# Another order for the steps of a fused attention and maxout kernel

## Chip, cores and metric

The kernel runs on one core of a Trainium2 chip. The time is the device time of one execution in microseconds. In the program one order of steps is written out by hand for all engines: TensorE (PE, with its weight loads as PEld), VectorE (DVE), ScalarE (ACT), GpSimd (POOL, here almost only an issuer of transfers) and SyncE (SP, an issuer of transfers).

## What is computed

Eight sequences of 448 positions go through attention with twelve heads of 64, and the result through a feed-forward block whose two branches are combined by a maximum.

```python
def _attn_ref(q, k, v, cap):            # (8, 12, 448, 64) each
    scores = q @ k^T / sqrt(64)
    scores = cap * tanh(scores / cap)
    attn = exp(scores - max);  attn = attn / (sum(attn) + 1e-9)
    return attn @ v

def _moe_ref(x, w1, w2, w_out):         # x: (3584, 768), w1, w2: (768, 1024)
    g = np.maximum(x @ w1, x @ w2)
    return g @ w_out                    # (3584, 768)
```

## The kernel before

**The arithmetic.** A maximum of two branches is h2 + relu(h1 - h2). So the kernel forms wd = w1 - w2 once on VectorE (steps `sub`) and wm = w2 · w_out once on TensorE (twelve products "premultiply", groups 0 to 11, from w2 transposed on TensorE by the steps W), and then computes relu(x · wd) · w_out + x · wm. Because tanh bounds the scores, exp is taken without a maximum.

**Tiles.** Four heads of one batch make a quad t; there are 24 quads, three for each batch. Quad 2 is cut into two parts of 256 and 192 queries, so there are 25 items n. Keys go in three tiles of 128 and a leftover of 64. Quads 0 to 4 are transposed on TensorE (steps X, copied by XC); quads 5 to 23 by the crossbar in a DMA that SyncE issues (`cr t`, line L373). kqs holds four quads of k and q as loaded, qkT three quads transposed, vp and vl four quads of v.

**The order.** One text, ORDER, lists 1,911 steps; each name stands for a function that issues one or more instructions. An engine takes its own instructions in the sequence in which they stand there, and waits in place for what they need; instructions of different engines are tied by semaphores alone. So the place of a step matters only among the steps of the same engine and queue. The steps:

| step | what it does | engine, line |
|---|---|---|
| lk, lq, lv, lw1, lw2, lwo | load k, q, v, the weights | POOL queue, L277, L284, L302, L317, L320, L307 |
| ld0, ld1, cd, cd1 | first loads of k and q, and their casts | SP and ACT queues; DVE, ACT |
| D | warming matmuls | PE L336 |
| X, Xh / XC | transposes on TensorE, and their copy to qkT | PE L365 / DVE L370 |
| W / WC | transposes of w2, and their copy | PE L344 / DVE L348 |
| cr t | crossbar transpose of quad t | SP queue, L373 |
| S n s z / T | scores of item n, sixth s, into PSUM slot z / tanh | PE L438 / ACT L447 |
| L n z / TL | leftover scores / their tanh | PE L456 / ACT L462 |
| E | exp, in place, of several tiles | ACT L469 |
| A, B | sums of exponentials over tiles | DVE L479, L484 |
| Y n bank / Yi 1 to 3 | totals / transpose, reciprocal, transpose | PE L497, L499, L502 / DVE L509, L512, L515 |
| VL, V | leftover values, values | PE L529, L539 |
| N n 0, N n 1 | normalise into xT | DVE L554, L558 |
| O g bank | group g takes a PSUM bank (no instruction) | |
| M x y n | n steps of groups x and y side by side | PE L582 |
| M x x n | n steps of group x on the whole array | PE L577 |
| H g | hand-over of group g | DVE queue, L590 |
| ev g | copy of a finished group out of PSUM | DVE L600, L613, L648, L651 |
| st b t | store of output tile t of batch b | SP and ACT queues, L622, L624, L629, L652 |

**Groups.** Group 12 and those behind it are stage 1 (x · wd, relu into gT) and stage 2 (gT · w_out + x · wm, copied to osb) of the batches in turn. In `M x y n` the two groups run in the upper and the lower 64 rows of the array at once; a group has to go through both halves, and between the two the kernel puts a hand-over, an empty instruction of VectorE that waits for the last matmul of the first half and is waited for by the first one of the second:

```python
    def hand_over(self, eng):
        self.turn = eng.nop().ins
        tc.add_manual_dep(self.turn, self.last[1].name, BANK, reason="bank")
```

The array works in different tilings: 64 x 128 for S and `M x y`, 64 x 32 for L and VL, 128 x 32 for Y and V, 64 x 64 for X, 128 x 128 for D, W and `M x x`.

**Buffers.** There are eight PSUM banks: two slots of two banks, z = 0 and 1, for scores and values (S, L and VL take them in turn; T, TL or N n 1 frees them), and four banks for groups, totals and transposes. Output tiles go through four buffers, `osb_all[:, (7 * (b // 2) + t) % OB, :DM]` with OB = 4, so a copy ev into one waits until the store of the tile four before has landed. `cr t` needs the buffer of qkT that was allocated three quads before, and quad t loaded in kqs.

**Ends.** ScalarE's work ends some 40 us before the kernel does; what is left then is stage 1 and 2 of the last batches on TensorE, with the last batch's 16 groups as `M x x`.

Of the kernel before, what the change touches and what calls it, by code (L numbers as in the profile page):

```python
# [14 lines left out]
lv 1 2; lq 6 0; lv 2 2; lw2 1; VL 0 1; W 2 2; WC 2; W 3 3; ev 1; WC 3; D 0 8; lq 5 0; E 0 1 0 2; E 0 0 0 3; Y 0 0;
Yi 0 1; Yi 0 2; Yi 0 3; lv 0 1; lv 0 0; lv 1 0; V 0 0; V 0 1; N 0 0; N 0 1; T 1 0; E 1 0 0 3; S 2 0 0; T 2 0;
E 1 1 2 4; E 1 1 0 2; O 2 2; O 3 1; M 2 3 8; H 3; H 2; lw2 2; W 4 3; WC 4; W 5 0; WC 5; M 3 2 3; lv 3 3; lk 5 0;
X 5 3; M 3 2 5; XC 5; S 2 1 0; lw1 0; sub 1 0; ev 3; L 2 1; TL 2; T 2 1; Y 1 0; Yi 1 1; Yi 1 2; sub 0 0; S 2 2 1;
T 2 2; E 2 1 0 2; O 4 3; O 5 1; M 4 5 8; H 5; lv 1 3; lv 1 1; VL 1 0; V 1 0; V 1 1; S 3 1 1; T 3 1; H 4; M 5 4 1;
ev 2; Yi 1 3; N 1 0; N 1 1; M 5 4 5; E 2 1 2 4; M 5 4 2; ev 5; S 3 0 1; T 3 0; lv 2 1; lq 8 0; lwo 1 0; O 6 0; O 7 2;  # L20
M 6 7 3; lk 6 0; M 6 7 1; lwo 1 1; M 6 7 2; S 3 2 0; T 3 2; M 6 7 2; H 7; H 6; ev 4; X 6 1; XC 6; L 3 1; TL 3;
E 3 1 0 2; lw1 1; sub 3 0; lk 10 0; lk 7 0; lv 3 2; lv 2 3; lv 2 0; lq 7 0; lk 8 0; lw1 2; lk 10 1; lq 10 0; lk 11 0;
lk 9 0; lk 11 1; lq 11 0; cr 5; lv 3 1; lq 9 0; lk 12 0; M 7 6 6; S 4 2 0; T 4 2; M 7 6 2; O 8 3; O 9 1; M 8 9 1;
ev 6; sub 2 0; ev 7; S 4 0 1; T 4 0; M 8 9 7; H 8; H 9; S 4 1 0; T 4 1; E 4 0 0 3; Y 2 0; Yi 2 1; Yi 2 2; VL 2 1;
X 7 2; XC 7; lk 12 1; lq 12 0; lk 13 0; lk 13 1; lq 13 0; lv 4 0; lv 4 1; lv 4 2; lv 4 3; lk 14 0; lv 3 0; lk 14 1;
lq 14 0; lk 15 0; lk 15 1; lq 15 0; X 8 0; XC 8; Yi 2 3; V 2 0; V 2 1; N 2 0; N 2 1; S 4 3 0; T 4 3; E 3 1 2 4;
M 9 8 8; ev 8; O 10 2; O 11 0; M 10 11 2; S 4 5 0; T 4 5; S 4 4 1; T 4 4; sub 5 0; M 10 11 6; H 11; H 10; sub 4 0;
ev 9; Y 3 3; Yi 3 1; S 5 2 0; T 5 2; M 11 10 4; S 5 0 1; T 5 0; M 11 10 4; Yi 3 2; ev 11; ev 10; L 4 0; TL 4; cr 6;
X 9 1; S 5 1 1; T 5 1; E 4 1 0 2; O 13 3; M 13 -1 2; O 14 0; M 13 14 4; O 17 2; M 17 14 2; XC 9; S 5 4 0; H 13;
M 17 13 3; H 14; M 17 13 1; M 14 13 2; VL 3 1; V 3 0; V 3 1; T 5 4; lv 5 0; lv 5 1; lv 5 2; lv 5 3; lk 16 0; lk 16 1;  # L30
lq 16 0; lk 17 0; lk 17 1; lq 17 0; lv 6 0; lv 6 1; lv 6 2; lv 6 3; lk 18 0; A 4 0 1; A 4 0 2; H 17; M 14 17 4; ev 13;
Yi 3 3; N 3 0; O 15 1; M 15 17 2; ev 17; O 19 3; M 15 19 4; H 15; N 3 1; E 4 1 2 4; L 5 0; TL 5; O 12 2; M 12 19 2;
H 19; M 12 15 4; H 12; M 19 15 2; ev 14; ev 15; A 4 1 1; S 5 3 1; T 5 3; E 5 1 0 2; M 19 12 4; ev 19; M -1 12 1;
O 18 0; M 18 12 1; O 16 1; M 18 16 5; H 18; M -1 16 1; H 16; S 5 5 0; cr 7; T 5 5; E 5 0 0 3; ev 12; M -1 18 1;
# [701 lines left out]
```

## Time and profile before

| | us |
|---|---|
| runs, median of 3 | 328.62 (328.51 to 330.5) |
| profiled execution, its own time | 329.16 |
| its span | 327.4 |
| TensorE busy | 319.1 (97%) |
| ScalarE busy | 274.5 (84%) |
| VectorE busy | 244.7 (75%) |
| GpSimd busy, nearly all of it issuing transfers | 163.5 (50%) |
| mean granted TensorE clock | 0.994 |

The span runs from the first to the last instruction; the execution's own time has 1.8 us around it. A busy row says that an instruction of the engine was under way, not that the engine ran at its peak. All times inside the span count from its start.

### The profile page before, as it was taken

To read this page: it belongs to the slowest core of one execution; us is meant where nothing else is said; L and a number is where in the kernel's file an instruction comes from. 1 tells how busy PE (TensorE), PEld (TensorE's weight loads), DVE (VectorE), ACT (ScalarE), POOL (GpSimd) and SP (SyncE) were. 2 spreads that over 40 slices of the span, in tenths; PEclk is the share of its full clock that TensorE was granted. 3 is DMA by queue.
4 is the path that set the end of the run, shared out by engine and by line. 5 is a ranking of instruction groups with operands and counts; after the bars stand their busy time and mean duration, and the time that the engine had idled before them with its cause. 6 is when DMAs were issued, how large, how long until landed. Compare 5 with 4: busy or idle time off the path is not lost.

```text
span 327.4 us, 10010 instructions
## 1 busy us (share of the span) xinstructions
PE 319.1 (97%) x4288; PEld 194.0 (59%) x4288; DVE 244.7 (75%) x447; ACT 274.5 (84%) x245; POOL 163.5 (50%) x241
## 2 busy tenths in 40 slices
PE   7799999999999999999999999999999999999995
PEld 7465567665546656555565565675567568555552
DVE  2349898988888688978888678889788777886213
ACT  3999999999999999999999998999899988900000
POOL 7567589998995865565577387543202000000000
PEclk9899999999999999999999999999999999999999
DMA  8999999999999999999999999996963006003034
GB/s 201 197 230 253 271 159 171 156 175 186 165 161 126 207 139 111 188 190 90 149 152 185 165 191 172 131 75 101 203 150 46 2 0 194 3 2 94 4 96 144
DMA packets 135083, 46.13 MB, mean 141 GB/s; under 512 B 116224, under 2 KB 130688, under 8 KB 134656
## 3 DMA queue, kind: packets, MB, share of 16 engines
q0 software_dynamic: 95168, 24.85, 76.9%
q1 hardware_dynamic: 39184, 19.40, 27.9%
q10 hardware_dynamic: 688, 1.25, 1.1%
q8 instruction: 33, 0.54, 0.7%
q14 instruction: 10, 0.08, 0.1%
HBM read 47.45 MB, written 11.01 MB: 179 GB/s over the span
## 4 chain that ended last, share of the span: by engine, by line
PE 94%; ACT 3%; DVE 2%; issue 0%; DVEq 0%
PE mm L582 59%; PE s L438 9%; PE s L539 9%; PE mm L577 8%; ACT e L447 2%; PE s L456 2%; PE s L529 2%; PE mm L502 2%; PE mm L336 2%; PE mm L365 1%; PE mm L497 1%; ACT e L469 0%; DVE xT L558 0%; PE mm L344 0%; ACT e L462 0%
## 5 line engine op out<-in xcount | busy, mean ns | idle before, releaser
L469 ACT ACTIVATE e<-e 128x1792 bf16<-128x1792 bf16 (+4 forms) x73 | 140.2, 1932 | 0.5
L447 ACT ACTIVATE e<-s 128x896 bf16<-128x896 f32 (+2 forms) x144 | 124.1, 935 | 6.0 <-PE s L438 5.7
L582 PE MATMUL mm<-wo_sb,gT 64*128 64x384 bf16 x768 | 95.8, 323 | 0.0
L582 PE MATMUL mm<-xT,wd_sb 64*128 64x448 bf16 (+2 forms) x768 | 79.9, 326 | 0.0
L582 PE MATMUL mm<-wm_sb,xT 64*128 64x384 bf16 x576 | 77.8, 323 | 0.0
L582 PEld LDWEIGHTS <-gT 64*128 64x128 bf16 x768 | 48.4, 94 | 23.3 <-issue 2.8
L302 POOL DMA_DIRECT2D vp<-in_v_dram x48 | 30.3, 637 | 60.6 <-PE s L539 29.0
L284 POOL DMA_DIRECT2D kqs<-in_k_dram x76 | 54.6, 721 | 9.7 <-DMA qkT<-kqs 3.1
L582 PEld LDWEIGHTS <-wd_sb 64*128 64x128 bf16 x768 | 46.3, 94 | 20.0 <-DVEq L590 2.4
L438 PE MATMUL s<-qkT 64*128 64x448 bf16 (+2 forms) x300 | 53.4, 346 | 2.6 <-ACT e L447 1.7
L582 PEld LDWEIGHTS <-xT 64*128 64x128 bf16 x576 | 38.2, 94 | 17.5 <-issue 2.2
L613 DVE TENSOR_SCALAR gT<-mm 128x448 bf16<-128x448 f32 (+2 forms) x72 | 38.9, 566 | 8.2 <-PE mm L582 4.4
L648 DVE COPY osb<-mm 128x384 f32<-128x384 f32 x54 | 28.4, 551 | 15.8 <-PE mm L577 11.5
L284 POOL DMA_DIRECT2D kqs<-in_q_dram x38 | 35.0, 921 | 1.5 <-DMA vl<-in_v_dram 0.7
L539 PE MATMUL s<-e,vp 128*32 128x448 bf16 (+2 forms) x600 | 32.1, 346 | 0.0
L558 DVE TENSOR_TENSOR xT<-s,inv 64x448 bf16<-64x448 f32 (+2 forms) x50 | 30.2, 603 | 2.4 <-PE mm L582 0.9
L479 DVE TENSOR_TENSOR esum<-esum,e 128x896 bf16<-128x896 bf16 x42 | 25.5, 618 | 7.8 <-PE mm L582 6.9
L438 PEld LDWEIGHTS <-qkT 64*128 64x128 bf16 x300 | 20.2, 94 | 18.6 <-issue 6.8
L302 POOL DMA_DIRECT2D vl<-in_v_dram x48 | 29.4, 622 | 0.3 <-DMA wo_sb<-in_moe_w_out_dram 0.3
L484 DVE TENSOR_TENSOR esum<-esum,e 64x896 bf16<-64x896 bf16 x42 | 26.0, 619 | 3.1 <-PE mm L582 0.8
L479 DVE TENSOR_TENSOR esum<-e 128x896 bf16<-128x896 bf16 x42 | 25.4, 617 | 2.9 <-PE mm L582 1.8
L509 DVE STREAM_TRANSPOSE st<-mm 128x448 f32<-128x448 f32 (+2 forms) x25 | 15.8, 630 | 13.3 <-PE mm L502 10.8
(54 smaller groups left out, 262.1 us busy)
## 6 DMA issues: line engine op xcount, KB each, us to landing
out_dram<-osb SPq DMA_DIRECT2D x51, 192.0 KB, 3.7
vp<-in_v_dram POOLq DMA_DIRECT2D x38, 160.0 KB, 4.9
kqs<-in_q_dram POOLq DMA_DIRECT2D x46, 112.0 KB, 4.9
kqs<-in_k_dram POOLq DMA_DIRECT2D x76, 56.0 KB, 4.3
osb<-in_moe_w_dram POOLq DMA_DIRECT2D x2, 1024.0 KB, 8.3
gT<-in_moe_w_dram POOLq DMA_DIRECT2D x3, 512.0 KB, 7.2
wo_sb<-in_moe_w_out_dram POOLq DMA_DIRECT2D x4, 384.0 KB, 7.0
w1l<-in_moe_w_dram POOLq DMA_DIRECT2D x1, 1024.0 KB, 5.2
```

Source lines behind the costliest of these rows:

```text
L284: nc.gpsimd.dma_start(out=to, in_=x)
L302: nc.gpsimd.dma_start(out=to, in_=x)
L438: nc.tensor.matmul(ps[:, h, x * w : (x + 1) * w], k_of(t, o, h, j), q_of(n, o, h))
L447: nc.scalar.activation(e, slots[n, s][:, :, :m], AF.Tanh, scale=scale / cap)
L469: nc.scalar.activation(e[:, j0 * m : hi], e[:, j0 * m : hi], AF.Exp, scale=float(cap))
L479: nc.vector.tensor_add(d, e[:, 0:2, :] if j == 1 else d, e[:, 2 * j : 2 * j + 2, :])
L539: nc.tensor.matmul(vals[n][R32[m], u, :w], vp[t % VB][:, x, j if turned_by_pe(t) else 2 * j, u::2], e_of(n, o, h, j), start=False, stop=(j ...
L558: nc.vector.tensor_mul(x[to], vals[n][r, 1, :w], sums[n, 3][to, :w])
L577: nc.tensor.matmul(self.ps, w, x, start=first, stop=self.at[0] == self.n)
L582: ins = nc.tensor.matmul(self.ps, w[r], x[r], start=first, stop=self.at == [self.n, self.n]).ins
L613: nc.vector.tensor_relu(gT[b // 2][:, f, cs], ps)
L648: nc.vector.tensor_copy(o[:, hs], ps)
```

## The change

Only the text ORDER is another; the functions are as they were. The new text has 1,904 entries, and stands for the same work: each load, transpose, score, exponential, sum, product, copy and store is there as often as before, and each group takes as many steps of M (some runs of M are split at other places, so that there are seven entries less). What differs is the sequence on each engine and queue, and which PSUM bank or slot a step uses. Compared as sequences, 142 of ScalarE's 246 entries, 213 of the POOL queue's 243 and 28 of SyncE's 47 stand in an unbroken common order. The quads in scores and values follow each other as before.

The start:

```diff
-ld0 k; ld0 q; ld1 k; ld1 q; lq 3 0; dm; D 0 32; D 0 8; ms0; cd k; lk 3 0; lw2 0; id; lv 0 3; lv 0 2; cd q; Xh 0 1 0;
-XC 0 1; cd1 q; Xh 0 0 1; XC 0 0; S 0 0 0; T 0 0; S 0 1 1; T 0 1; X 3 2; S 0 2 0; cd1 k; X 1 3; T 0 2; XC 3; S 1 3 1;
-T 1 3; XC 1; S 0 5 0; T 0 5; S 1 4 1; T 1 4; L 0 0; TL 0; S 0 3 1; T 0 3; E 0 1 2 4; lwo 0 1; lq 2 0; W 1 0; WC 1;
-S 1 5 0; S 0 4 1; T 0 4; T 1 5; lk 2 0; X 2 1; XC 2; W 0 2; S 1 2 1; T 1 2; S 1 1 0; T 1 1; lq 4 0; lk 4 0; X 4 3;
+ld0 k; ld0 q; dm; D 0 32; D 0 8; ld1 k; ld1 q; lq 3 0; lk 3 0; lq 2 0; lw2 0; ms0; id; lk 2 0; lq 4 0; cd k; Xh 0 0 0;
+XC 0 0; cd q; cd1 q; Xh 0 1 1; XC 0 1; S 0 1 0; T 0 1; S 0 2 1; T 0 2; cd1 k; X 1 2; X 3 3; S 0 0 0; T 0 0; XC 1;
+S 0 4 1; T 0 4; S 0 3 0; T 0 3; XC 3; S 1 5 1; T 1 5; S 0 5 0; T 0 5; L 0 1; TL 0; E 0 1 2 4; X 2 0; XC 2; S 1 4 0;
+T 1 4; S 1 3 1; T 1 3; W 1 1; WC 1; W 0 2; WC 0; S 1 0 0; T 1 0; E 0 1 0 2; lwo 0 0; lk 4 0; X 4 3; XC 4; lv 1 2;
...
```

SyncE's queue of transposes and stores, taken out of the two texts:

```diff
-cr 5; cr 6; cr 7; cr 8; st 0 0; cr 9; cr 11; cr 10; st 0 1; st 0 2; cr 12; st 1 4; st 1 3; st 1 6; cr 13; cr 14;
-st 1 5; st 2 0; cr 15; cr 16; cr 17; st 2 1; st 2 2; cr 18; st 3 3; st 3 5; cr 20; st 3 4; cr 19; st 4 1; st 3 6;
-cr 21; cr 22; st 4 0; st 4 2; cr 23; st 5 5; st 5 4; st 5 3; st 5 6; st 6 2; st 6 0; st 7 3; st 6 1; st 7 5; st 7 4; st 7 6
+cr 5; cr 6; cr 7; cr 8; st 0 0; cr 9; cr 10; st 0 1; st 0 2; cr 11; cr 12; cr 13; st 1 6; cr 14; st 1 4; st 1 3;
+cr 15; st 1 5; st 2 0; cr 16; st 2 1; cr 17; st 2 2; st 3 3; st 3 6; st 3 5; cr 18; cr 19; st 3 4; cr 20; st 4 0;
+cr 21; cr 22; cr 23; st 4 1; st 4 2; st 5 4; st 5 6; st 5 3; st 5 5; st 6 1; st 6 2; st 6 0; st 7 3; st 7 4; st 7 5; st 7 6
```

Around output tile (2,2), groups 62 and 63, whose buffer of osb held tile (1,5):

```diff
+T 13 2; O 63 1; M 58 63 2; O 62 3; M 62 63 3; S 13 1 0; T 13 1; E 13 0 0 3; lv 12 3; lk 30 0; lk 30 1; lq 30 0;
+lk 31 0; lk 31 1; lq 31 0; st 1 3; ev 59; ev 58; cr 15; st 1 5; M 62 63 9; VL 12 1; L 14 0; st 2 0; Y 12 0; Yi 12 1;
...
+N 12 1; M 63 61 5; S 14 1 0; T 14 1; M 63 61 7; H 61; M 63 62 2; A 13 0 1; ev 63; A 13 1 1; S 14 5 1; cr 16; T 14 5;
+M 61 62 4; S 14 2 0; T 14 2; M 61 62 4; S 14 0 1; T 14 0; M 61 62 4; ev 62; E 13 1 2 4; O 67 0; M 61 67 2; ev 61;
```

And the last item of attention:

```diff
-M 121 -1 2; ev 121; H 118; ev 123; lv 23 1; lv 23 2; lv 23 3; VL 24 0; V 24 0; Y 24 0; Yi 24 1; Yi 24 2; V 24 1;
-Yi 24 3; N 24 0; N 24 1; M 122 118 14; O 124 3; M 124 124 6; O 125 0; M 125 125 1; ev 122; st 6 2; M 125 125 5;
+VL 24 0; B 24 0; B 24 1; Y 24 3; N 23 0; N 23 1; ev 121; st 6 1; H 118; V 24 0; V 24 1; H 122; M 122 118 14; Yi 24 1;
+Yi 24 2; Yi 24 3; N 24 0; N 24 1; O 124 1; M 124 124 6; O 125 3; M 125 125 1; ev 124; ev 122; st 6 2; M 125 125 5;
...
```

More of the change, by code (lines that the diff above doesn't have):

```diff
@@ L15 @@
[L15 to L34, printed above, removed]
@@ new lines @@
+sub 3 0; M 7 6 7; S 4 0 1; T 4 0; M 7 6 1; ev 6; ev 7; S 4 2 0; T 4 2; O 8 0; O 9 3; M 8 9 7; S 4 1 1; T 4 1;
+E 4 0 0 3; M 8 9 1; sub 2 0; lk 8 0; lq 8 0; lq 7 0; lk 10 0; lv 2 1; lk 7 0; lk 10 1; lq 10 0; lw1 2; lk 9 0;
+lk 11 0; lk 11 1; lq 11 0; cr 5; Y 2 2; Yi 2 1; VL 2 0; X 7 1; X 8 2; V 2 0; V 2 1; Yi 2 2; Yi 2 3; H 8; H 9; XC 7;
+S 4 5 1; T 4 5; XC 8; N 2 0; N 2 1; E 3 1 2 4; M 9 8 8; O 10 1; O 11 2; M 10 11 1; ev 8; M 10 11 2; S 5 2 0; T 5 2;
+S 4 4 1; T 4 4; sub 5 0; M 10 11 5; H 10; H 11; sub 4 0; Y 3 0; Yi 3 1; ev 9; S 5 0 0; T 5 0; M 11 10 4; S 4 3 1;
@@ new lines @@
+T 4 3; M 11 10 4; ev 10; ev 11; L 4 0; TL 4; lq 9 0; lk 12 0; lk 12 1; lv 3 0; lq 12 0; lk 13 0; lv 3 3; lk 13 1;
+lq 13 0; lv 4 0; cr 6; lv 3 2; lv 3 1; lv 4 1; lv 4 2; lv 4 3; lk 14 0; lk 14 1; lq 14 0; lk 15 0; lk 15 1; lq 15 0;
+lv 5 0; lv 5 1; X 9 0; XC 9; S 5 1 1; T 5 1; E 4 1 0 2; O 13 3; M 13 -1 2; O 14 1; M 13 14 4; H 13; O 17 2; M 17 14 2;
+H 14; Yi 3 2; Yi 3 3; S 5 4 0; M 17 13 4; H 17; A 4 0 1; M 14 13 2; ev 13; VL 3 1; V 3 0; V 3 1; T 5 4; N 3 0;
+A 4 1 1; M 14 17 4; O 15 0; M 15 17 2; ev 17; O 19 3; M 15 19 4; H 15; N 3 1; E 4 1 2 4; L 5 0; TL 5; O 12 2;
@@ new lines @@
+M 46 44 3; S 9 4 0; T 9 4; M 46 44 4; S 9 2 1; T 9 2; A 8 0 1; A 8 1 1; ev 37; A 8 0 2; ev 41; A 8 1 2; M 46 44 3;
+S 9 1 0; T 9 1; M 46 44 3; H 44; O 42 1; M 46 42 1; H 46; S 9 0 1; T 9 0; E 9 0 0 3; M -1 42 1; M 44 42 6; VL 8 0;
+L 10 1; B 8 0; B 8 1; Y 8 2; V 8 0; V 8 1; TL 10; Yi 8 1; Yi 8 2; Yi 8 3; N 8 0; lv 10 1; lv 10 2; lv 10 3; lk 26 0;
+lk 26 1; lq 26 0; lk 27 0; lk 27 1; M 44 42 6; H 42; M 44 46 1; N 8 1; M 44 46 1; E 9 1 0 2; S 10 5 1; cr 12; T 10 5;
+M 42 46 9; S 10 2 0; T 10 2; M 42 46 3; A 9 0 1; ev 44; A 9 0 2; ev 46; O 47 2; M 42 47 1; S 10 0 1; T 10 0;
@@ new lines @@
+S 11 4 1; E 10 1 2 4; M 45 51 1; S 11 0 0; T 11 0; H 51; A 10 1 2; B 10 0; B 10 1; T 11 4; E 11 1 0 2; M 45 43 10;
+ev 45; M 51 43 1; VL 10 0; V 10 0; V 10 1; Y 10 0; Yi 10 1; Yi 10 2; L 12 1; TL 12; M 51 43 3; ev 43; O 50 2;
+M 51 50 2; O 54 0; M 54 50 1; ev 51; S 12 0 1; T 12 0; M 54 50 3; O 55 1; M 54 55 1; H 50; M 54 55 1; M 50 55 2;
+S 12 4 1; M 50 55 2; Yi 10 3; H 54; M 50 54 2; A 11 1 1; H 55; N 10 0; ev 50; M 55 54 4; ev 54; O 56 3; M 55 56 2;
+ev 55; O 53 2; M 53 56 4; H 56; O 57 0; M 53 57 2; M 56 57 4; E 11 0 0 3; T 12 4; E 11 1 2 4; S 12 5 1; T 12 5;
@@ new lines @@
+O 52 1; M 56 52 2; lq 27 0; cr 13; lv 11 0; lv 11 1; lv 11 2; lv 11 3; lk 28 0; lk 28 1; lq 28 0; lk 29 0; st 1 6;
+lk 29 1; lq 29 0; cr 14; lv 12 0; lv 12 1; lv 12 2; N 10 1; S 12 2 0; T 12 2; H 57; M 57 52 4; S 12 3 1; T 12 3; H 53;
+M 57 53 2; A 11 0 1; B 11 0; H 52; M 52 53 1; S 12 1 0; T 12 1; E 12 0 0 3; ev 56; ev 57; M 52 53 3; O 60 3;
+M 52 60 2; O 59 0; M 59 60 1; A 11 0 2; A 11 1 2; ev 52; B 11 1; ev 53; VL 11 1; L 13 0; V 11 0; V 11 1; TL 13;
+Y 11 1; Yi 11 1; Yi 11 2; Yi 11 3; M 59 60 11; H 60; S 13 0 0; O 58 2; M 59 58 2; M 60 58 1; A 12 0 1; H 59; N 11 0;
@@ new lines @@
+S 15 1 0; T 15 1; M 72 73 2; S 15 0 1; T 15 0; M 72 73 3; M 72 -1 1; S 15 3 0; T 15 3; E 15 0 0 3; ev 66; M 72 73 5;
+ev 71; M 72 73 1; O 76 0; M 76 73 2; VL 14 1; L 16 0; V 14 0; V 14 1; TL 16; A 14 1 1; A 14 1 2; B 14 1; B 14 0; H 72;
+A 14 0 2; Y 14 2; Yi 14 1; Yi 14 2; M 76 72 11; Yi 14 3; M 76 72 1; H 73; M 73 72 2; S 16 5 0; H 76; M 73 76 3;
+N 14 0; N 14 1; ev 72; M 73 76 7; E 15 1 0 2; T 16 5; E 15 1 2 4; A 15 1 1; S 16 4 0; T 16 4; S 16 3 1; M 73 76 1;
+T 16 3; M 73 76 1; ev 73; O 77 2; M 77 76 1; st 2 2; st 3 3; M 77 76 1; O 78 1; M 77 78 6; S 16 0 0; T 16 0;
@@ new lines @@
+H 86; O 84 2; M 84 83 2; M 84 86 4; O 87 3; M 87 86 2; E 17 1 0 2; T 18 2; N 16 1; H 84; H 83; A 17 1 1; ev 86;
+S 18 0 1; M 87 84 1; S 18 3 0; M 87 84 3; M 83 84 2; H 87; M 83 87 1; E 17 1 2 4; A 17 1 2; B 17 1; B 17 0; T 18 0;
+T 18 3; S 18 4 1; T 18 4; E 18 1 2 4; M 83 87 2; VL 17 0; lk 38 0; lk 38 1; lq 38 0; lk 39 0; V 17 0; V 17 1; ev 84;
+Y 17 1; Yi 17 1; cr 18; L 19 1; TL 19; E 18 0 0 3; M 83 87 1; ev 83; O 88 2; M 88 87 2; O 92 1; M 88 92 1; ev 87;
+Yi 17 2; Yi 17 3; M 88 92 4; S 19 1 1; M 88 92 2; T 19 1; M 88 92 5; O 90 0; M 90 92 2; H 88; M 90 88 4; N 17 0;
@@ new lines @@
+N 17 1; M 90 88 8; H 92; H 90; E 18 1 0 2; A 18 1 1; A 18 0 1; B 18 1; S 19 5 1; T 19 5; S 19 4 0; T 19 4; M 92 88 2;
+ev 88; M 92 90 6; S 19 0 1; T 19 0; M 92 90 4; S 19 2 0; T 19 2; M 92 90 2; ev 92; O 91 3; M 91 90 2; S 19 3 1;
+T 19 3; E 19 1 0 2; E 19 0 0 3; O 89 2; M 91 89 12; lk 39 1; lq 39 0; lv 17 0; lv 17 1; cr 19; st 3 4; L 20 0;
+lv 17 2; lv 17 3; lk 40 0; lk 40 1; VL 18 1; lq 40 0; lk 41 0; lk 41 1; lq 41 0; cr 20; lv 18 0; lv 18 1; lv 18 2;
+lv 18 3; lk 42 0; lk 42 1; lq 42 0; lk 43 0; lk 43 1; lq 43 0; lv 19 0; B 18 0; A 18 1 2; A 18 0 2; Y 18 1; V 18 0;
@@ new lines @@
+V 18 1; TL 20; ev 90; Yi 18 1; Yi 18 2; H 91; Yi 18 3; N 18 0; O 93 0; M 93 89 2; H 89; M 93 91 3; N 18 1; M 93 91 9;
+H 93; M 89 91 1; S 20 4 0; M 89 91 1; ev 91; M 89 93 3; S 20 5 1; M 89 93 6; E 19 1 2 4; T 20 4; T 20 5; S 20 1 0;
+T 20 1; M 89 93 3; O 97 1; M 97 93 1; A 19 0 1; A 19 0 2; A 19 1 1; S 20 3 1; T 20 3; ev 89; st 4 0; M 97 93 1;
+O 95 3; M 97 95 2; S 20 2 0; T 20 2; M 97 95 1; B 19 1; B 19 0; M 97 95 1; H 97; O 99 2; M 99 95 1; S 20 0 1; T 20 0;
+M 99 95 1; H 95; M 99 97 4; H 99; A 19 1 2; M 95 97 2; ev 97; ev 93; VL 19 0; L 21 1; V 19 0; Y 19 1; Yi 19 1;
@@ new lines @@
+S 22 3 1; T 22 3; M 102 108 3; S 22 0 0; T 22 0; M 102 108 5; H 108; O 105 3; M 102 105 1; S 22 2 1; T 22 2;
+E 22 0 0 3; M 102 105 1; lv 20 1; lv 20 2; lv 20 3; VL 21 0; lk 46 0; lk 46 1; lq 46 0; lk 47 0; V 21 0; lk 47 1;
+lq 47 0; cr 23; st 4 1; ev 107; lv 21 0; lv 21 1; lv 21 2; lv 21 3; lv 22 0; lv 22 1; lv 22 2; lv 22 3; lv 23 0;
+A 21 1 2; Y 21 0; Yi 21 1; Yi 21 2; Yi 21 3; V 21 1; N 21 0; S 23 4 1; T 23 4; M 108 105 12; H 102; M 108 102 1;
+H 105; M 108 102 1; S 23 5 1; N 21 1; st 4 2; ev 108; M 105 102 9; S 23 3 0; M 105 102 3; O 106 0; M 105 106 1;
@@ new lines @@
+ev 125; O 126 1; M 126 126 6; ev 126; ev 118; st 6 0; O 127 0; M 127 127 6; O 128 3; M 128 128 6; O 129 1;
+M 129 129 6; O 130 2; M 130 130 1; ev 129; M 130 130 5; ev 130; O 131 1; M 131 131 6; O 132 2; M 132 132 9; ev 127;
+M 132 132 1; ev 128; M 132 132 3; ev 131; M 132 132 1; O 133 0; M 133 133 14; ev 133; O 134 3; M 134 134 14; ev 132;
+st 7 3; O 135 1; M 135 135 14; O 136 0; M 136 136 14; O 137 2; M 137 137 10; ev 134; ev 135; st 7 4; M 137 137 4;
+ev 136; ev 137; st 7 5; O 138 3; M 138 138 14; ev 138; O 139 1; M 139 139 14; ev 139; st 7 6;
```

205 lines of the change are left out of this document (82 added, 123 removed).

## The prediction

> **What bounds the kernel now.** I read the page first, then the busy time by stages, the timeline at the end of the start-up, the waits, SyncE's own timeline, and the chain at the end.
>
> ```profile
> span 327.4 us, 10010 instructions
> ...
> PE 319.1 (97%) x4288; PEld 194.0 (59%) x4288; DVE 244.7 (75%) x447; ACT 274.5 (84%) x245; POOL 163.5 (50%) x241
> ...
> PE   7799999999999999999999999999999999999995
> ...
> ACT  3999999999999999999999998999899988900000
> ...
> PE 94%; ACT 3%; DVE 2%; issue 0%; DVEq 0%
> ```
>
> TensorE is busy 97% of the span, ScalarE until about 284 us. A busy PE row is modelled, so I also took the distance from each matmul's start to the next and subtracted its columns at full speed (187 ns for 448). The columns make 288.3 us of the 327.4 by that count.
>
> ```profile
> 0.00:30.80 30.80, 26.37 (x432) 17.89 (x432) 14.04 (x30) 25.79 (x24) 20.52 (x39) 0.94 1.15 217
> 30.80:64.00 33.20, 33.20 (x632) 21.11 (x626) 29.47 (x57) 32.70 (x33) 27.88 (x40) 1.00 1.50 195
> 64.00:160.00 96.00, 95.99 (x1295) 56.72 (x1293) 79.57 (x145) 94.94 (x86) 72.04 (x101) 1.00 1.44 157
> 160.00:256.00 96.00, 95.97 (x1266) 57.39 (x1264) 78.70 (x141) 93.50 (x84) 43.01 (x62) 1.00 1.14 141
> 256.00:296.00 40.00, 40.00 (x522) 25.34 (x518) 32.11 (x58) 27.59 (x23) 0.00 (x0) 1.00 0.15 41
> ```
>
> The columns after the stage's limits are length, then busy PE, PEld, DVE, ACT, POOL, and near the end the granted clock. In the first row TensorE sits idle in places and its clock falls; in the others it never does. So there are two regimes, and the next lines show where one ends.
>
> ```profile
> 27.59 3.27 ACT L469 ACTIVATE e<-e 128x1792 bf16<-128x1792 bf16 x2
> ...
> 30.87 0.79 PE L497 MATMUL mm<-e,ones 128*32 128x448 bf16 x12
> ```
>
> The matmul at 30.87 is Y 1: it waits for the exponentials that end there. Until then ScalarE sets the time: from its first tanh at 7.39 it has no gap over 0.15 us. By Y 1 TensorE has done 16.56 us of columns and lost 13.3 us beside its start at 0.99. From there to the last matmul it loses 20.7 us: 13.1 us in 96 changes of the array's tiling (0.137 us each, mostly S or M to L, L to V, V to M), and 7.6 us in 555 steps that follow without a change. In this last part the waits that can be named are few:
>
> ```profile
> PEld L582 <- DVEq L590: 4.0, 19, 0.5
> ...
> PE s L438 <- ACT e L447: 1.7, 5, 0.4
> ```
>
> Weight loads run ahead of matmuls, so the first line is not lost matmul time. From starts, 19 scores after 30.8 us came late, 1.9 us together.
>
> **The change, part by part.** Every step is there as often as before; only the sequence, and the banks and slots, differ. No duration changes, so the sum is one of waits and tiling changes.
>
> *Start-up.* The same 21 tanh and exponential steps stand ahead of Y 1 on ScalarE, and the same 16.56 us of columns on TensorE. Added from 7.39 us (0.80 us from start to start for a tanh of 896, 1.59 for an exponential of 1792, 2.34 for 2688) they end at 30.6 us in both orders. The first scores still need both halves of quad 0 transposed, at 5.59 after 40 warming matmuls that end at 5.44. One more load stands ahead of the identity on the POOL queue: 3.09 becomes about 3.66 us, 1.6 us before its use. I take 0; bounds -0.1 (the chain before waited up to 0.12 us for copies of transposes) and +0.6 (cover gone: one load's issue).
>
> *Tiling changes.* From Y 1 on I count 97 before and 95 after (leftover scores L stand more often next to VL). 2 x 0.137 = **-0.27 us**. The 24 half-empty steps ("M -1 y n") and 49 pairs of unequal width are the same.
>
> *Scores against ScalarE.* By the same addition, the lag of TensorE behind its columns that ScalarE forces at most is, in stretches of 20 us of columns, 14.0, 16.8, 19.2, 20.8, 21.9, 22.5 before and 14.0, 16.8, 19.2, 20.8, 21.7, 22.4 after; for the stretch at 220 it is 24.2 and 24.3. TensorE's true lag is 1.2 us above that at 47 us, 4 at 146 and 8.7 at 265. So scores can wait no more than before; 0, bounds -1.9 (all 19 late scores on time) and +1.9 (as many again).
>
> *Crossbar transposes.* Nineteen move on SyncE's queue; two swaps (11 before 10, 20 before 19) go. The shortest distance from readiness in the queue to first use grows from 11.5 to 14.4 us of columns.
>
> ```profile
> 103.05 1.30 SPq L373 DMA_TRANSPOSE qkT<-kqs  x1
> 104.39 2.70 SPq L629 DMA_DIRECT2D out_dram<-osb  x4
> ```
>
> But before, the tightest one (15) landed at 168.04 for scores at 173.37, 5.3 us early, and no wait of TensorE names one. A longer lead of something early is worth 0, both ways.
>
> *Loads.* The POOL queue keeps its 236 transfers. Put at the landing times that the same places of the queue had before, each early load still lands 2.0 us or more ahead of its transposes or values (1.1 before). 0.
>
> *VectorE.* Hand-overs H (124) have the same shortest lead after the start-up, 160 ns of matmuls, and bank reuse 293 ns; the 23 slots that pass from values to scores have 1.95 us (1.97 before). Near the end N 23 now stands behind B 24, so after Y 24 VectorE has ev 121, Yi 24 and N 24 to do, 0.55 + 0.63 + 0.24 + 0.65 + 0.62 + 1.26 = 3.95 us, from about 0.5 us after Y 24; TensorE reaches the last input of that at 0.56 + 0.56 + 2.24 + 0.93 + 0.3 = 4.6 us. This just fits; 0, bounds 0 and +0.5 (one more operation in between).
>
> *Stores.* This is what the order pays with: stores now stand behind transposes. Of output tile (1,5) the store is issued behind transpose 15, and tile (2,2) needs its buffer. Transpose 15 can go at 149 us; with 1.3 to 3 us of issue the store goes at 151 to 153 and lands 4 to 6 us later, 155 to 158.7 (in the lines above the first stores landed at 110.66 and 111.12, just after transpose 10 at 109.43). The copy ev 63 into that buffer is ready at 155.3 and VectorE waits in order. Behind it are A 13, ev 62, ev 61; TensorE needs the bank of ev 62 at 159.23, which holds while the landing is before 157.4. Value 0 (middle 156.5), bounds 0 and +1.3.
>
> [...]
>
> *End.*
>
> ```profile
> 296.21 27.40 PE mm L577 x160
> ...
> 323.64 0.42 DVE osb L651
> ```
>
> Batch 7's products run in one piece, and the last copy and store follow; both orders end in the same way with the same 3.8 us after the last matmul. 0.
>
> **Sum.** -0.27 us on the profiled execution's own 329.16 us (span 327.4, 1.8 us around it): 328.9. That execution lies 0.54 us above the median of the runs, 328.62; on that median it is **328.3 us**.
>
> **The rivals.**
> (a) *The late scores vanish.* For it: 19 late scores and ScalarE's gaps of up to 0.7 us, a few of which another order can close. Against: the forced lag is the same. 328.3 - 1.3 (two thirds of 1.9) = 327.0.
> (b) *A store holds VectorE* (slower): place ev 63 at 155 us, price up to 1.3 us, deciding from a landing after 157.4. For it: after a transpose, tile (0,2)'s second store took 6 us from issue to landing; against: the queue is idle before 149. 328.3 + 1.3 = 329.6; a little slower than before.
> (c) *The clock falls twice* (slower). The granted clock was 0.51 from 13.1 to 16.6 us, after a stretch (9.8 to 13.1) with 1.80 us of busy PE in 3.30. The new order has transposes X 2 in the first of these stretches where W 1 was, and W 1 in the second. If the clock stays low to 20.0 us, the 2.0 us of columns there take twice as long, with 0.5 us of cover: 328.3 + 1.5 = 329.8.
> [...]
> (d) *Scores come later than I count*: more waits on ScalarE or VectorE at many places. 19 late scores twice over and (b): 328.6 + 1.9 + 1.3 = 331.8. Against: every lead I compared is equal or longer.
> That the change does not do what it says is part of the forecast: it protects transposes for which nothing waited.
>
> **How the numbers follow.** Forecast 0.55, (a) 0.18, (b) 0.12, (c) 0.06, (d) 0.09. A measurement of this kernel tells about 1% (3.3 us) from no change. Faster than 325.3 needs more than all late scores: 0.04, from the far end of (a). Slower than 331.9 needs (d) or several costs at once: 0.08. Within 1%: 0.88. The range holds the forecast, (a), (b), (c): all but part of (d) and the far end of (a), 326.8 to 330.8.
>
> **What would show it.** After: Y 1 within 0.3 us of 30.87; no wait of TensorE on a qkT transfer, as before; 95 tiling changes behind it; ScalarE's last operation at 283 to 285 us; the row of L577 x160 again at 27.4 us; at 155 us a wait of VectorE for a store, under 2 us. I am wrong if the row of the first 30.8 us is longer by over 0.5 us, if the granted clock is low in a second stretch, or if TensorE's waits on DVE or ACT after 31 us grow by over 2 us.

## The result, and the profile after

The changed kernel took 328.34 us (median of 20 executions, 327.62 to 329.36), the kernel before 329.33 us in the 20 beside them (328.21 to 331.43); the ratio is 0.9968, with a 95% interval of 0.9954 to 0.9982. Measured a second time (e11 below) the ratio was 0.9973 (0.9960 to 0.9985). So the new order is faster by 0.3%, which is real and small. The functions are the same; lines of the changed kernel are two lower than before (L438 is L436, L582 is L580).

The page of the changed kernel, as far as it answers to the lines of before:

```profile
span 326.8 us, 10006 instructions
...
PE 317.8 (97%) x4288; PEld 193.3 (59%) x4288; DVE 245.1 (75%) x447; ACT 274.2 (84%) x245; POOL 163.8 (50%) x241
...
PE 92%; ACT 5%; DVE 2%; issue 0%; DVEq 0%
```

The span is 0.6 us shorter and TensorE is busy 1.3 us less; VectorE, ScalarE and the POOL queue stay within 0.4 us. By stages (length, then busy PE, PEld, DVE, ACT, POOL, then the granted clock, and last the busy share of the transfers and their GB/s):

```profile
0.00:30.80 30.80, 25.73 (x436) 17.45 (x440) 13.72 (x30) 25.87 (x24) 20.56 (x39) 0.94 1.14 215
30.80:64.00 33.20, 33.16 (x627) 21.23 (x624) 29.91 (x57) 32.97 (x32) 27.30 (x40) 1.00 1.49 198
64.00:160.00 96.00, 95.94 (x1297) 56.97 (x1294) 79.57 (x146) 95.35 (x87) 72.89 (x102) 1.00 1.55 165
```

The same two regimes: gaps and a lowered clock in the first row, a full TensorE behind it. Where they meet, on the timeline:

```profile
28.82 1.74 ACT L467 ACTIVATE e<-e 128x1792 bf16<-128x1792 bf16 x1
...
30.69 0.75 PE L495 MATMUL mm<-e,ones 128*32 128x448 bf16 x12
```

Y 1 stands at 30.69 instead of 30.87. The waits that can be named are as small as before, and the chain ends in the same way:

```profile
PEld L580 <- DVEq L588: 3.5, 18, 0.4
...
PE s L436 <- ACT e L445: 2.0, 5, 0.4
```

```profile
295.65 27.40 PE mm L575 x160
323.06 0.02 issue
323.08 0.42 DVE osb L649
```

So from Y 1 to the end of the last matmul it is 292.73 us before (30.87 to 323.60) and 292.35 after (30.69 to 323.04). I call this distance the body. Of the 0.56 us between the two last matmuls 0.18 lie ahead of Y 1 and 0.38 in the body. The medians differ by 0.99, more than the two profiled executions do (329.16 and 328.59). That difference needed an explanation: the times of the kernel before look like two heaps, 11 of the 20 from 328.2 to 329.4 and 9 from 330.2 to 331.4, while the changed kernel has one.

### The profile page after: what moved, and what is told of

The parts are those of the page before. It is cut to its first block, busy times and chain, and to the rows that moved or that the text cites. A ratio compares the mean times of both kernels' runs of the same rounds, so it can differ in the third digit from the quotient of the medians.

```text
span 326.8 us, 10006 instructions
## 1 busy us (share of the span) xinstructions
PE 317.8 (97%) x4288; PEld 193.3 (59%) x4288; DVE 245.1 (75%) x447; ACT 274.2 (84%) x245; POOL 163.8 (50%) x241
## 4 chain that ended last, share of the span: by engine, by line
PE 92%; ACT 5%; DVE 2%; issue 0%; DVEq 0%
PE mm L580 58%; PE s L537 9%; PE s L436 8%; PE mm L575 8%; ACT e L445 3%; PE s L527 2%; PE s L454 2%; ACT e L467 2%; PE mm L500 2%; PE mm L334 1%; PE mm L363 1%; PE mm L495 1%; DVE xT L556 0%; ACT e L460 0%; DVE w2T L346 0%
## 5 line engine op out<-in xcount | busy, mean ns | idle before, releaser
L445 ACT ACTIVATE e<-s 128x896 bf16<-128x896 f32 (+2 forms) x144 | 123.4, 931 | 7.3 <-PE s L436 7.2
L580 PE MATMUL mm<-wo_sb,gT 64*128 64x384 bf16 x768 | 94.5, 323 | 0.0
L580 PE MATMUL mm<-xT,wd_sb 64*128 64x448 bf16 (+2 forms) x768 | 80.2, 326 | 0.0
L580 PE MATMUL mm<-wm_sb,xT 64*128 64x384 bf16 x576 | 77.7, 323 | 0.0
L580 PEld LDWEIGHTS <-gT 64*128 64x128 bf16 x768 | 49.7, 94 | 21.6 <-issue 1.5
L580 PEld LDWEIGHTS <-wd_sb 64*128 64x128 bf16 x768 | 44.2, 94 | 22.7 <-DVEq L588 2.9
L436 PE MATMUL s<-qkT 64*128 64x448 bf16 (+2 forms) x300 | 53.3, 346 | 2.7 <-ACT e L445 2.0
L580 PEld LDWEIGHTS <-xT 64*128 64x128 bf16 x576 | 38.7, 94 | 16.3 <-issue 2.6
L646 DVE COPY osb<-mm 128x384 f32<-128x384 f32 x54 | 29.4, 554 | 17.6 <-PE mm L575 9.9
L436 PEld LDWEIGHTS <-qkT 64*128 64x128 bf16 x300 | 20.9, 94 | 17.6 <-issue 6.8
L460 ACT ACTIVATE e<-s 128x896 bf16<-128x896 f32 (+2 forms) x25 | 22.2, 889 | 2.5 <-PE s L454 2.0
```

What stands on the lines that cost most here:

```text
L436: nc.tensor.matmul(ps[:, h, x * w : (x + 1) * w], k_of(t, o, h, j), q_of(n, o, h))
L445: nc.scalar.activation(e, slots[n, s][:, :, :m], AF.Tanh, scale=scale / cap)
L580: ins = nc.tensor.matmul(self.ps, w[r], x[r], start=first, stop=self.at == [self.n, self.n]).ins
L646: nc.vector.tensor_copy(o[:, hs], ps)
```

## The experiments

Three theories. SUM: the small gains of the two profiles, ahead of Y 1 and behind it, stand in every execution and add up. CLOCK: the upper heap comes from the start-up, where the granted clock falls at a time that differs from one execution to the next (at 13.15 us in the profile of before, at 11.91 in that of the changed kernel), and the new start avoids it. LATE TRANSFERS: the upper heap comes from transposes, loads or stores that land late in the body, and the new order has more lead for them.

**e1: the kernel before, again.** No edit.

> The kernel before, unchanged, to learn its spread. Both theories: ratio 1.000 within its interval. Theory SUM (the 0.6 us of the two profiles, 0.2 in the start-up and 0.35 behind it, stand in every execution): the runs make one hump of about 1.5 us width, 328.2 to 329.7, and the nine runs above 330.1 of the twenty seen so far are a chance that does not come back. Theory CLOCK (some executions of the kernel before lose 2 us more because the granted clock falls at a bad place in the start-up): again two humps, 328.2 to 329.4 and 330.2 to 331.4, with about 4 runs of 10 in the upper one, and the long executions show a lower mean granted clock (0.987 or less where the short ones have 0.993). Theory LATE TRANSFERS: two humps as well, with the same clock in both.

Measured: ratio 1.000 (0.9985 to 1.0015); its 12 executions lay from 328.72 to 330.36. The 35 of the kernel before that ran beside them had 12 between 329.88 and 330.74. The upper heap does come back, against SUM as far as it goes. But the executions of the upper heap do not share one mean clock: six show 0.988, the others 0.993 to 0.995, and the lower heap has 0.990 to 1.000. So the mean clock does not sort them, and this form of CLOCK fell. The profile of e1 holds more: its clock rose at 4.52 us (6.32 in the first profile) and was at 0.5 from 11.35 to 18.17, twice as long, and yet Y 1 came at 30.86.

**e2 and e3: one half of the new order at a time.** The steps of one text up to Y 1, then the rest of the other without what the head has done.

In e2 the seam is this (new above, old below):

```diff
 M 3 2 5; ev 2; ev 3; S 2 1 1; L 2 0; TL 2; T 2 1; lw1 0; sub 0 0; ...
+Y 1 0; Yi 1 1; Yi 1 2; S 2 2 1; T 2 2; E 2 1 0 2; O 4 3; O 5 1; M 4 5 8; ...
```

And in e3 (old above, new below):

```diff
 S 2 1 0; lw1 0; sub 1 0; ev 3; L 2 1; TL 2; T 2 1; ... ev 2; sub 0 0;
+Y 1 1; Yi 1 1; Yi 1 2; O 4 3; O 5 0; M 4 5 1; S 2 2 0; T 2 2; E 2 1 0 2; ...
```

> The new order up to the totals Y 1 (30.8 us), and the old order from there. SUM: the start-up's share alone, -0.2 us, ratio 0.9994. CLOCK: the upper hump goes with the old head, so the whole gain of about -1 us in the medians is here, ratio 0.997, no run above 329.6. LATE TRANSFERS: the upper hump stays, some runs of ten at 330 to 331.4.

> The old order up to the totals Y 1, and the new order from there. SUM: the share behind 30.8 us alone, -0.35 us, ratio 0.999. CLOCK: the upper hump stays (some runs of ten 1.5 to 2 us above the rest), ratio 0.999. LATE TRANSFERS: the upper hump goes, ratio 0.997, all runs within 1.7 us.

Measured: e2 1.0021 (1.0006 to 1.0036), e3 1.0016 (1.0000 to 1.0031). Neither half alone gains anything, which no theory expected. The seam is to blame, as their profiles show: in e2 S 2 2 asks for the slot that S 2 1 had just taken and starts 1.43 us behind Y 1 instead of 0.91 in the kernel before, 0.52 late; in e3 Y 1 asks for a bank whose copy ev 3 stands behind the subtraction `sub 1 0` on VectorE, and comes at 31.95, after an idle time of 0.96 us. Halves of two orders that were each made as a whole do not fit at a cut. The bodies can still be read: e2's (old) is 293.25, which is 292.73 without that one late score, and e3's (new) is 292.30.

The heaps are in both. Of e2's 12 executions nine lay from 329.68 to 329.99 and three higher (330.56, 330.62, 331.17); of e3's nine from 329.23 to 329.79 and three higher (330.52, 330.89, 331.03). CLOCK had expected no such executions with the new start of e2, LATE TRANSFERS none with the new rest of e3. Neither half by itself does away with the long executions.

**e4: warming matmuls in the start-up.**

```diff
-S 0 5 0; T 0 5; S 1 4 1; T 1 4; L 0 0; TL 0; S 0 3 1; ...
+D 1 5; S 0 5 0; T 0 5; D 1 5; S 1 4 1; T 1 4; D 1 5; L 0 0; TL 0; D 1 5; S 0 3 1; ...
```

> The kernel before with four steps of five warming matmuls (0.27 us each at full clock) put into TensorE's idle places between 9.5 and 12.4 us, ahead of scores that wait for ScalarE; nothing else differs. CLOCK: the granted clock no longer falls to 0.5 at 13 us, the start-up is up to 0.5 us shorter (Y 1 at 30.4 to 30.9), the mean clock is 0.998 or more and there is no upper hump; ratio 0.996 to 0.997. SUM and LATE TRANSFERS: the matmul work of the lowered stretch was hidden under ScalarE, so Y 1 stays within 0.15 us of 30.87 and the ratio is 1.000; under LATE TRANSFERS the upper hump stays.

Measured: 1.0013 (0.9993 to 1.0033), 328.53 to 331.15. In the profile the clock does not fall in the start-up (it rose at 6.16), and Y 1 stands at 30.85, the body is 292.67. The low clock of before, 3.41 us from 13.15 on, is hidden under ScalarE, as SUM said: Y 1 stood at 30.87 with it. The upper heap stayed: four of the 12 took over 330 us, three of them with a span of 328.6 or 328.7. The fourth has a span of 327.4 and lost its time outside the span, which in e4 leaves 1.7 to 2.8 us around it (1.7 to 1.9 in all other runs).

**e5 and e6: the halves with a better seam,** at O 2 (25.4 us), the bank of Y 0 renamed to what the rest expects.

```diff
 e5: new head ... Y 0 0 (was Y 0 1) ... then, from O 2 2; O 3 1 on, the old rest
 e6: old head ... Y 0 1 (was Y 0 0) ... then, from O 2 0; O 3 2 on, the new rest
```

> The new order up to the second pair of groups (about 25.4 us), the old order from there; the seam lies earlier than in e2, where S 2 2 had to wait for a slot (0.5 us of TensorE at 32 us, a fault of the seam and not of either order). Bank of Y 0 as in the old order, so that the rest finds the banks it had. SUM: -0.2 us of the start-up alone, ratio 0.9994, a profile with Y 1 at 30.7 and a last matmul at 323.4. CLOCK: the upper hump is gone, ratio 0.997. LATE TRANSFERS: the upper hump stays.

> The old order up to the second pair of groups, the new order from there; the bank of Y 0 as in the new order (in e3 Y 1 had to wait 0.96 us for a bank, a fault of the seam). SUM: -0.35 us, ratio 0.999, a profile with Y 1 at 30.9 and a last matmul at 323.2. CLOCK: upper hump stays. LATE TRANSFERS: the upper hump is gone, ratio 0.997.

Measured: e5 0.9999 (0.9982 to 1.0016). Its profile is of an execution of 410.7 us (span 408.9, mean clock 0.75) and can't be set beside the others; the other eleven reach 330.05, three of them from 329.98 on. So e5 is inconclusive. e6 0.9995 (0.9977 to 1.0012), five of 12 executions above 329.6. But the profile of e6 caught a long execution: span 328.5. The old start in it, in windows of 3.41 us (length, busy PE, granted clock, then the busy share of the transfers and GB/s):

```profile
10.26:13.68 3.42, 2.12 (x24) 1.00 1.28 200
13.68:17.09 3.41, 2.94 (x40) 0.50 1.30 201
17.09:20.50 3.41, 3.23 (x48) 0.50 1.25 188
20.50:23.92 3.42, 3.30 (x46) 1.00 1.29 193
```

The clock is low for two windows, to 20.50. In the profile of before it was low for one, to 16.56. What that does to the first products (before first, then e6), and to ScalarE in e6:

```profile
18.39 2.35 PE L582 MATMUL mm<-wo_sb,w2T 64*128 64x384 bf16 x22
```

```profile
19.15 3.00 PE L580 MATMUL mm<-wo_sb,w2T 64*128 64x384 bf16 x22
21.89 0.45 PE L436 MATMUL s<-qkT 64*128 64x448 bf16 x2
...
25.27 0.75 PE L495 MATMUL mm<-e,ones 128*32 128x448 bf16 x12 [0.35 <-DVE wm_sb L598]
...
32.58 0.75 PE L495 MATMUL mm<-e,ones 128*32 128x448 bf16 x12
```

```profile
19.29 0.92 ACT L460 ACTIVATE e<-s 128x896 bf16<-128x896 f32 x1 [0.45 <-PE s L454]
...
27.71 1.02 ACT L445 ACTIVATE e<-s 128x1024 bf16<-128x1024 f32 x1 [0.30 <-PE s L436]
...
32.72 0.60 ACT L460 ACTIVATE e<-s 128x512 bf16<-128x512 f32 x1 [0.82 <-PE s L454]
```

The same 22 matmuls take 3.00 us instead of 2.35 and start 0.76 later. From then on ScalarE, which otherwise sets the time here, waits for scores, and Y 1 comes at 32.58: 1.71 us later than in the profile of before. Of these, 1.41 us stand already at the score at 21.89 (20.48 before), just behind the low stretch. The other 0.3 come at Y 0, which waits 0.35 us for a copy out of the bank that the edit gave it, so they belong to the seam. The body is 292.14, no longer than in a short execution. So this long execution is made ahead of Y 1, by the clock for 1.4 us of it, and LATE TRANSFERS does not explain it.

**e7 and e8: two more profiles of the kernel before.** No edit.

> One more profile of the kernel before, for an execution in the upper hump (a chance of about 3 in 10). If it is one: CLOCK expects the granted clock at 0.5 for 6.8 us from 13 to 14 us on, a Y 1 at 32 us or later, and the same offsets from there to the end; LATE TRANSFERS expects Y 1 at 30.9 and a step of 1 to 2 us somewhere behind it, at a wait for a transfer.

> The same as e7, one more look at the kernel before: in an execution of the upper hump CLOCK expects a Y 1 at 32 us or later with the clock low for 6.8 us, LATE TRANSFERS a step of 1 to 2 us behind 31 us at a wait for a transfer.

Measured: 328.97 and 328.91, both short. Y 1 at 30.66 and 30.64, bodies 292.74 and 292.71. In e8 the clock was low for two windows as well, but from 11.00 to 17.82, early enough to be covered. So in these profiles it is not the length of the low stretch that costs (6.82 us in e8, 6.83 in e6), it is how far it reaches into the products behind 18 us: to 20.50 in e6, with Y 1 at 32.58. Neither profile met a long execution, so no long execution of the kernel before itself was profiled.

**e9 and e10: warming matmuls in all the gaps,** in the kernel before and in the changed one. e9's edit is this, e10's is its like (D 0 4 and D 3 4 ahead of nine steps from S 0 4 to S 1 0).

```diff
+D 1 4; S 0 2 0; ... D 1 4; S 0 5 0; ... D 1 4; S 1 4 1; ... D 1 4; L 0 0; ... D 1 4; S 0 3 1; ...
+D 1 5; S 0 4 1; ... D 0 4; S 1 2 1; ... D 0 5; S 1 1 0; ...
```

> The kernel before with eight warming steps (4 or 5 matmuls each) in TensorE's idle places from 8.3 to 17.2 us, so also behind those of e4, where in e4 the window from 12.99 to 16.40 had only 2.10 us of busy TensorE. CLOCK: no execution has the clock low for 6.8 us any more, none is above 330, and the spread shrinks to that of the first tanh (6.8 to 7.45 us); median 328.7 to 329.0, ratio 0.998 to 0.9995, since only the upper third of the executions gains. SUM, LATE TRANSFERS: the upper third stays, ratio 1.000; the extra matmuls delay scores by up to 0.3 us.

> The changed kernel with nine warming steps (4 or 5 matmuls each) in TensorE's idle places from 8.5 to 16.3 us. CLOCK: the executions with a long low clock (329.3 us) go, median 328.0 to 328.4, ratio to the kernel before 0.995 to 0.997; the start-up is bound by ScalarE from its first tanh, so the best execution stays at 327.6. If the extra matmuls push scores behind ScalarE's need: Y 1 at 30.9 to 31.2 and a ratio of 0.998.

Measured: e9 0.9996 (0.9983 to 1.0009), e10 0.9986 (0.9969 to 1.0003): no gain over what each was made from, and both still have executions 1 us above the rest (330.27; 329.74, 329.82, 330.93). Both profiles caught one, and show a second kind that I had not thought of. e9, windows and the timelines of TensorE and ScalarE, and one line of ScalarE in e10:

```profile
3.61:7.03 3.42, 2.79 (x46) 1.00 1.16 270
7.03:10.44 3.41, 3.41 (x62) 1.00 1.24 192
```

```profile
5.59 0.95 PE L365 MATMUL mm<-ident,kqs 64*64 64x64 bf16 x28
...
8.78 0.61 PE L336 MATMUL mm<-warm 128*128 128x128 bf16 x4
9.32 0.55 PE L438 MATMUL s<-qkT 64*128 64x448 bf16 x2
...
7.63 1.73 ACT L447 ACTIVATE e<-s 128x896 bf16<-128x896 f32 x2 [1.90 <-PE s L438]
9.92 0.92 ACT L447 ACTIVATE e<-s 128x896 bf16<-128x896 f32 x1 [0.56 <-PE s L438]
```

```profile
10.12 2.54 ACT L446 ACTIVATE e<-s 128x896 bf16<-128x896 f32 x3 [0.77 <-PE s L437]
```

The clock rises at 10.44 instead of 4.2 to 6.9. The column shows 1.00 ahead of the first recorded rise, but the 28 transposes take 0.95 us there and 0.63 at full clock. The window before, 3.61 to 7.03, ends in the wait for the first copies of transposes and has 2.79 us of busy TensorE; no rise came at its end, and one came at the end of the next, which has 3.41. ScalarE's first tanh comes at 7.63 and its third only at 9.92 (7.62 and 10.12 in e10). Y 1 stands at 32.07 in e9 and at 32.12 in e10, the bodies are 292.67 and 292.08. In e10 the late tanh is made ahead of the first extra matmul (10.0 us): 0.44 us at the first tanh against e11 and 0.77 of idle time ahead of the third make 1.2 of the 1.3 us by which Y 1 is later than in e11. The fillers came too late for it. In e9 the late first tanh lies ahead of them too, but the first four extra matmuls, at 8.78, stand ahead of the score at 9.32 that the third tanh waits for, and take up to 0.54 us of that wait.

**e11: the changed kernel again.** No edit.

> The changed kernel, unchanged. All theories: ratio 0.9968 as measured (0.9954 to 0.9982). CLOCK: Y 1 somewhere between 29.9 and 31.5 by where the clock's windows fall, but from Y 1 to the end of the last matmul 292.35 us as in its first profile, within 0.1 (the kernel before: 292.70 to 292.73). LATE TRANSFERS: that distance varies by 0.5 us or more from one profile to the next. No execution above 329.7.

Measured: 0.9973 (0.9960 to 0.9985), 327.86 to 329.27. Y 1 at 30.80, body 292.08, so 0.27 less than in the first profile, more than the 0.1 that I had allowed. Of this, 0.20 us lie at one place, the change from groups 8 and 9 to 10 and 11. The first profile has an idle time in its weight loads there that e11 has not (first profile, then e11):

```profile
45.64 0.76 PEld L580 LDWEIGHTS <-w2T 64*128 64x128 bf16 x11 [0.27 <-issue]
```

```profile
44.55 1.75 PEld L580 LDWEIGHTS <-w2T 64*128 64x128 bf16 x22
```

The profile shows nothing that it waited for, so the cause stays open. e10 has not got it either, and its body is 292.08 too.

**e12: twenty more changes of tiling.**

```diff
-O 22 3; M 16 22 1; ...
+D 3 1; O 22 3; M 16 22 1; ...        (and so ahead of O 28, 38, 48, 53, 69, 77, 80, 90, 100)
```

> The changed kernel with one warming matmul (128 x 128, 53 ns of columns) put between two products of the 64 x 128 tiling at ten places from 50 to 240 us: twenty tiling changes more. By the prediction's price of 0.137 us each, if TensorE has no slack there: from Y 1 to the last matmul 292.35 + 10 x (0.053 + 2 x 0.137) = 295.6 us. If a change is hidden by other waits: 292.9 (the columns alone).

Measured: body 295.29, span 329.6. Against 292.08 to 292.35 that is 2.9 to 3.2 us more, where 3.3 was expected. Step by step: all steps with a change lose 16.38 us instead of 12.89, and the columns add 0.53, together 4.0; but the products ahead of scores lose 2.35 instead of 3.15, since TensorE, being later, waits less for ScalarE: scores that start over 0.06 us late behind a product are 12 instead of 17. So 73 to 80% of what is put on TensorE here comes out at the end.

The profiles side by side (times in us; e2 and e3 with the seams told above, and without e5 and e12):

| order of start / rest | clock rises | low clock | first tanh | Y 1 | body |
|---|---|---|---|---|---|
| old / old, before | 6.32 | 13.15 to 16.56 | 7.39 | 30.87 | 292.73 |
| old / old, e1 | 4.52 | 11.35 to 18.17 | 6.81 | 30.86 | 292.70 |
| old / old, e7 | 5.39 | 12.22 to 15.63 | 7.18 | 30.66 | 292.74 |
| old / old, e8 | 4.17 | 11.00 to 17.82 | 6.64 | 30.64 | 292.71 |
| old / old, e4 | 6.16 | none | 7.36 | 30.85 | 292.67 |
| old / old, e9 | 10.44 | none | 7.63 | 32.07 | 292.67 |
| new / old, e2 | 4.87 | 11.70 to 15.11 | 6.97 | 30.86 | 293.25 |
| old / new, e3 | 6.59 | 13.42 to 16.83 | 7.44 | 31.95 | 292.30 |
| old / new, e6 | 6.85 | 13.67 to 20.50 | 7.44 | 32.58 | 292.14 |
| new / new, after | 5.09 | 11.91 to 15.33 | 7.07 | 30.69 | 292.35 |
| new / new, e11 | 5.33 | 12.15 to 15.57 | 7.18 | 30.80 | 292.08 |
| new / new, e10 | 10.45 | none | 7.62 | 32.12 | 292.08 |

The last column is the result in one view: 292.67 to 292.74 with the old rest (292.73 in e2 without its late score), whatever happened at the start, and 292.08 to 292.35 with the new one, 0.3 to 0.65 less.

## Why the prediction was right, and where not

**The sum.** The forecast was two changes of tiling less and nothing else. From Y 1 on the traces have 96 changes before and 94 after (97 and 95 were counted), and the steps with a change lose 13.16 us and 12.90 (12.89 in e11): 0.26 less, against -0.27 forecast. By e12 73 to 80% of such time reaches the end. The term that was mis-sized is the steps that follow without a change of tiling, taken as equal: they lose 7.58 us before, 7.47 after and 7.21 in e11. This is 0.1 to 0.4 us more gain. Products behind products lose 2.45 us before, 2.37 and 2.18 after. Leftover scores and leftover values that follow each other lose 0.41 before and 0.22 in both after: three places that lost 128, 85 and 42 ns before (at 60.6, 115.1 and 243.3 us) have no like, none there loses over 14 ns now. Products ahead of scores go the other way, 3.00 us before, 3.22 and 3.15 after. So it isn't the late scores. Those over 0.06 us late behind a product are 17 before (1.87 us in all), 18 after (2.17) and 17 in e11 (2.03), so rival (a) did not come; nor did rival (d).

**The base.** The forecast of 328.3 stands near the measured 328.34 in part by luck. It was the sum on a median of three runs, 328.62. Over all executions measured here the kernel before has a median of 329.11 (121 of them), the changed one 328.45 (32). The gain between these is 0.66 us, more than twice the forecast one: with the executions above 329.85 left out, the kernel before has 329.01, so 0.56 us of it are in the ordinary executions, about what the bodies differ by (0.3 to 0.65), and some 0.1 comes from the long ones.

**The start-up.** Forecast 0, Y 1 within 0.3 of 30.87: it came at 30.69 and 30.80, inside the 30.64 to 30.87 of the old order's short executions. Right. What the prediction did not see is that Y 1 is not one number. Rival (c), a second low window, was priced at 1.5 us and put down to the new order. The kernel before has it too (e1 and e8, unharmed), and so has the old start in e6, where it cost 1.4 us in the way that (c) gives: columns at a granted clock of 0.50, with too little cover. The 20.0 us in (c) was an estimate, a second stretch as long as the first, that no run had shown by then; in e6 the low clock lasted to 20.50. The new order seems to have it as well, an estimate from its mean clocks, since no profile of it shows two windows. Its profiles with one low window show 0.993 and 0.994, while nine of its 32 executions show 0.987 or 0.988, as e6 with two does. These nine took 327.62 to 328.65 us, so it did no harm there. One step was wrong although the forecast held: the time of the low window was read as a property of the order, from one execution.

**Transposes.** No wait of TensorE names a crossbar transpose, as forecast, and as before. The leads are more even: transposes 10, 13 and 15 landed 5.7, 7.9 and 5.3 us ahead of their first scores and now 15.3, 19.1 and 21.2. But the shortest is not longer, against what I counted: transpose 18 stands behind the stores of (3,6) and (3,5), landed at 204.49, and is used at 209.00, 4.5 us later (7.2 in e11). It costs nothing either. In these runs more lead for transposes bought no time.

**Stores.** Of rival (b) nothing came. SyncE's queue and VectorE in the changed kernel at that place:

```profile
150.11 2.52 SPq L627 DMA_DIRECT2D out_dram<-osb  x4
...
155.32 0.56 DVE L646 COPY osb<-mm 128x384 f32<-128x384 f32 x1
155.79 0.61 DVE L477 TENSOR_TENSOR esum<-e 128x896 bf16<-128x896 bf16 x1
157.39 1.02 DVE L646 COPY osb<-mm 128x384 f32<-128x384 f32 x2 [0.98 <-PE mm L580]
```

The copy ev 63 starts at 155.32 with no idle time ahead of it. The two parts of the store (1,5) landed at 154.55 and 155.02, 0.3 us before, where I had put 155 to 158.7: transpose 15 landed at 151.97 already, 3.4 us after its issue, against 9.8 us for the same one before. The estimate of the landing was too late. The wait of VectorE at 155 us that was named as a sign did not come, by 0.3 us; by the bound of the prediction itself (a landing after 157.4) a cost would have needed 2.4 us more. The store landed behind the transpose here too, as in the rows that the forecast went by.

**The end.** The row of L575 x160 has 27.40 again, and 3.8 us follow it. ScalarE's last operation was forecast for 283 to 285 us; it ended at 287.87, because the leftover scores of the last item stand later and its tanh starts at 283.04. TensorE needs its result only at 291.5, so this miss had no price.

**What stays open.** The changed kernel had no execution above 329.36 in 32, the one before had 36 above 329.85 in 121. Two causes of long executions are shown, both in the clock of the first 21 us, in edited kernels: a low clock that lasts to 20.5 us (e6) and a late first rise (e10, and with its fillers e9). How many of the 36 they make is not known. Of the 27 whose mean clock is on record, ten show 0.987 to 0.989, near e6's 0.988, and one 0.999, which is e9's; the other sixteen, 0.984 and 0.993 to 0.995, are like no long execution that was profiled. A late rise with one low window of 3.41 us behind it would give about 0.995, an estimate from 3.41 us at 0.50 in a span of 328, but no profile shows that. That the new start is proof against long executions is not shown: e10 is the same program up to its first extra matmul and fell into the late rise, and e2, with the new start, had three of 12. Nor are executions independent draws: of the 35 of the kernel before beside e1 six lay within 0.14 us of each other, all with a mean clock of 0.988.

## What to carry to other kernels

When a kernel is measured to tenths of a per cent, cut its trace where one regime ends and compare the part behind the cut alone: here that distance repeats to 0.1 us with the old order and 0.3 us with the new one, while Y 1 differs by 1.9 us between profiles with the old start. Before a change in an order is priced, ask whether anything waits for what it protects: nothing waited for transfers that were already 5 us early, so no gain is seen from longer leads, while two changes of the array's tiling less took 0.26 us off TensorE's losses. And judge neither half of an order by cutting it in two: the seams of e2 and e3 cost more than the whole change was worth.

## What the runs showed of the hardware

In the start-up the changes of the granted clock lay 3.41 us apart, or twice that: in the profile of before it rose at 6.32 us, fell 6.83 later, at 13.15, and rose again 3.41 after that, at 16.56. The windows above are stretches of 3.41 us counted from these changes. Their place against the kernel's start differs from execution to execution. The first rise was at 4.17 (e8) to 6.85 us (e6) in most profiles, and at 10.44 (e9) and 10.45 us (e10) in two, where the window that ended at 7.03 or 7.04 had 2.79 us of busy TensorE and no rise came at its end (in e6 one came behind a window with 2.96). That is a spread of 2.7 us, and of 6.3 with the two late rises. The falls came behind windows with 1.46 (e11) to 2.13 us (e1) busy; in e4 none came behind a window with 2.10. Behind lowered windows with 2.98 (e1), 2.94 (e6) and 3.08 us busy (e8) the clock stayed low for another one; behind the others, which had 3.12 us or more, and 2.99 in e12, it rose. So the busy time of a window does not by itself tell in these runs what the clock did next. The mean clock that goes with a run does not show a late rise: it is 0.999 in e9 and 1.000 in e10, although the 28 transposes at 5.59 us took 0.95 us in both and 0.63 in e11.

Where TensorE waits for nothing, on the whole array (L577 in the profile of before), the next matmul starts 109 ns after one of 256 columns, 189 after one of 448 and 216 after one of 512: 0.417 to 0.418 ns for each further column, at which columns are counted here.
